# Gaps of 32 bytes between the weight blocks and between the x and g tiles of a fused attention and MLP kernel

## The chip, the core and the metric

The kernel runs on one core of one Trainium2 chip. The metric is the device time of one execution in microseconds; the kernel before has a median of 677.18 us over 3 runs (677.18 to 677.52). The instruction profile is of one further execution, which has a span of its own.

## What is computed

Sliding-window attention with sink tokens (4 batches, 8 heads, 768 positions, head dimension 64, 4 sinks, window 128), and behind it an MLP of 512 by 2048 with a leaky activation, over all 3072 tokens, in float32:

```python
scores = scale * np.matmul(q, k.transpose(0, 1, 3, 2))
keep = is_sink | in_window                    # rel = query - key position, 0 <= rel < window
scores = np.where(keep, scores, -1000000000.0)
a = np.exp(scores - max); a = a / (sum(a) + 1e-09)
x = np.matmul(a, v)                           # heads laid side by side: 3072 x 512
h = x @ w_in                                  # 512 x 2048
g = np.maximum(h, 0.0) + alpha * np.minimum(h, 0.0)
out = g @ w_out                               # 2048 x 512
```

## The kernel before, in words

The 3072 tokens are cut into 12 chunks of 256 (`NCHUNK`, three to a batch). The MLP's inner dimension of 2048 is cut into 16 blocks of 128, `f` = 0 to 15 (`NF`).

Each weight block f is one tile of 8192 bytes a partition in the memory of the core. It arrives as 64-bit floats in 32-bit words (`load_weights`), and is turned (`convert_weights`) into four parts of 512 float32 columns: high and low part of w_in, and high and low part of w_out. The converted block takes the place of the raw one (the same `tag`), so a block lies where its load was put. All 16 blocks stay in memory to the end. The memory of the last three (f = 13, 14, 15) is first lent to the input tiles of chunk 0 and to small tables, and is handed to the weights later; the dictionary `lent` names these three.

Attention of a chunk leaves its output transposed in two tiles, `xh` (its high part) and `xl` (the rest), each of 4 x 256 columns. There are two of each kind, used in turn by the chunks.

The MLP of a chunk goes through its 16 blocks:
- `gemm1(c, f)`, line L894: twelve matmuls of 256 columns. For each of four slices of the 512 inputs, w_in's high part is multiplied with xh and with xl, and its low part with xh. The weights are the stationary operand, x is the moving one. The result is in a PSUM bank.
- the activation: ACT scales the bank by alpha (L898), DVE takes the larger of the two (L899) into `g`, ACT rounds it into `gh` (L900), DVE writes the rest to `gl` (L901). There are three tiles each of gh and gl, used in turn by the blocks.
- `gemm2(c, f)`, lines L931, L932 and L929: six matmuls of 512 columns. Here gh or gl (128 columns of it) is the stationary operand and w_out's parts are the moving one: for each of the two halves of the tokens, gh with w_out's high part (L931) and its low part (L932), then for each half gl with the high part (L929). They add into two PSUM banks, over all 16 blocks.

`gemm2` runs two blocks behind `gemm1` (`LAG`). The attention of the next chunk is spread over the first twelve blocks of the present one, between its products; its scores are the matmuls L597 and L598. The last chunk has no attention beside it. Ahead of its block f = 8, the function `judge` begins, a test of whether the inputs allow this fast path; a single transpose of it is on TensorE (L1048).

The order of the instructions on each engine is made when the kernel is built: `Plan.draw` simulates the engines with estimated costs, and `Plan.issue` emits the operations in that order. Costs and order don't depend on where tiles lie.

Memory of the core is handed out by two pools, `const` (weights and what stays to the end) and `main` (`pool` in the code, all else of the fast path), in the order in which tiles are first asked for, each tile in one run of bytes, the same in every partition. A tile's place is then the sum of the sizes before it, each rounded up to 32 bytes. The helper `several` asks for the n tiles of a kind.

The places of the operands of the two products in the kernel before, modulo 128 bytes: the weight blocks 32, but 64 for f = 14; xh, xl, g, gh and gl all 96.

Of the kernel before, what the change touches and what calls it, by code (L numbers as in the profile page):

```python
# [3 lines left out]

# [5 lines left out]
F32 = mybir.dt.float32  # L10
F32R = mybir.dt.float32r
# [8 lines left out]
P = 128  # L20
# [4 lines left out]
QC = 2 * P  # L25
# [4 lines left out]
KT = DM // P  # L30
LAG = 2
# [47 lines left out]
class Plan:  # L79
# [20 lines left out]
    def held(self, tile_):  # L100
        v = Value(None)
        v.at = tile_
        return v

    def op(self, engine, cost, run, reads=(), writes=(), tail=0.09, mode=None, nbytes=0, other=None, locks=False):
        o = Op(engine, cost, tail, run, self.rank if engine == "PE" else None)
        o.ways = {engine: (cost, run)}
        if other:
            o.ways[other[0]] = other[1:]
        o.born = self.rank  # L110
        if engine == "PE":
            self.rank += 1
        o.mode, o.nbytes, o.index = mode, nbytes, len(self.ops)
        seen = []
        for group, writing in ((reads, False), (writes, True)):
            for x in group:
                v, key = x if isinstance(x, tuple) else (x, None)
                if v not in seen:
                    seen.append(v)
                keys = [k for k in set(v.wrote) | set(v.read) if key is None or k is None or k == key]  # L120
                for k in keys:
                    o.before.update(v.wrote.get(k, ()))
                    if writing:
                        o.before.update(v.read.get(k, ()))
                if writing:
                    for k in keys:
                        if key is None or k == key:
                            v.wrote.pop(k, None)
                            v.read.pop(k, None)
                    v.wrote.setdefault(key, []).append(o)  # L130
                else:
                    v.read.setdefault(key, []).append(o)
        for v in seen:
            v.left += 1
        o.values = seen
        o.takes = [v for v in seen if v.kind]
        o.locks = locks
        self.ops.append(o)
        return o
# [182 lines left out]
def program(ctx, tc, qk, pairs, vp, vq, vs, w, par, out):  # L322
    nc = tc.nc
    const = ctx.enter_context(tc.tile_pool(name="const", bufs=1))
    fast = ctx.enter_context(ExitStack())
    pool = fast.enter_context(tc.tile_pool(name="main", bufs=1))
    psum = ctx.enter_context(tc.tile_pool(name="psum", bufs=1, space=bass.MemoryType.PSUM))
    plan = Plan(tc)
# [3 lines left out]
    for name, which in (("s", (0, 1)), ("pa", (2, 3)), ("h", (4, 5)), ("o", (6, 7))):  # L332
        plan.kind(name, [banks[i] for i in which])

    def several(name, n, shape, dtype):
        plan.kind(name, [pool.tile(shape, dtype, name=f"{name}{i}") for i in range(n)])

    scratch = ctx.enter_context(tc.tile_pool(name="scratch", bufs=1, space=bass.MemoryType.DRAM))
    plan.kind("swap", [scratch.tile([4, P, P], F32, name=f"swap{i}") for i in range(2)])
    plan.kind("turns", [scratch.tile([4, P, 2 * 32], F32, name=f"turns{i}") for i in range(2)])  # L340
    trid = held(scratch.tile([P, 2, P], F32, name="trid"))
    several("stage", 2, [P, QC + KC], F32)
    several("kq", 2, [P, KC + 2 * QC], F32R)
    several("v", 4, [P, 3, 2, D], F32)
    several("pt_", 3, [P, 2, WIN], F32)
    several("comb", 5, [P, 4 * P], F32)
# [7 lines left out]
    several("sinkT", 1, [P, QC], F32R)  # L354
    several("vs", 1, [P, DM], F32R)
    several("ob", 2, [P, DM], F32)
    several("xh", 2, [P, KT, QC], F32R)
    several("xl", 2, [P, KT, QC], F32R)
    several("g", 2, [P, QC], F32)
    several("gh", LAG + 1, [P, QC], F32R)  # L360
    several("gl", LAG + 1, [P, QC], F32R)

    size = const.tile([P, NF], F32, name="size")
    sizes = held(size)
# [2 lines left out]
    def load_weights(f, engine="ACT"):  # L367
        raw = raws[f] = held(None)

        def run():  # L370
            raw.at = const.tile([P, 2 * DM, 2], I32, tag=f"w{f}", name="wraw")
            (nc.sync if engine == "SP" else nc.scalar).dma_start(
                raw.at.rearrange("p (i x) w -> p i (x w)", i=2), w[f].bitcast(I32).rearrange("i p x -> p i x"))
        return op(engine, ISSUE if engine == "SP" else 0.12, run, writes=[raw] + lent.get(f, []), nbytes=8 * P * 2 * DM)
# [35 lines left out]
    lent = {}  # L410
# [136 lines left out]
    xh, xl, prep, comb, sink, ptile_, sums, rinv, nms, wt = {}, {}, {}, {}, {}, {}, {}, {}, {}, {}  # L547
# [730 lines left out]
```

## Time and profile before

| | |
|---|---|
| median of 3 runs | 677.18 us |
| profiled execution, span | 676.2 us |
| TensorE matmul busy | 663.8 us (98%), 4532 matmuls |
| weight loads busy (beside the matmuls) | 580.5 us (86%), 4534 |
| VectorE busy | 525.8 us (78%) |
| ScalarE busy | 397.5 us (59%) |
| mean granted TensorE clock | 0.994 |
| DMA | 85.19 MB, 126 GB/s in the mean |

A share of busy time counts an instruction from its start to its end. Matmuls overlap on TensorE: the next starts while the one before is still draining, so the sum of their durations is larger than the time they take up, and the pace is read from the distance of their starts. In the page's rows "bank<-xh,w" stands for a matmul that writes a PSUM bank and reads x and w; "x1536" is the count; behind the bar stand busy microseconds, the mean nanoseconds of one, and the idle time before them with what ended it. PEld rows are the loads of the stationary operand. In a timeline row the first number is the start in microseconds from the start of the span, the second the time to the end of what the row merges, and "x1" the count of instructions.

### The profile page before, as it was taken

The page shows a single profiled execution, that of the slowest core. Times are in us where ns is not written, and L with a number is a line of the kernel's source. Part 1 is how long each engine was busy: PE and PEld are TensorE (multiplying, and loading weights), DVE is VectorE, ACT ScalarE, POOL GpSimd, SP SyncE. Part 2 cuts the span into 40 slices and gives each one's busy share as a digit, 9 for nine tenths or more (in the row PEclk, how much of TensorE's full clock was granted, in tenths as well). Part 3 has the DMA queues.
Part 4 walks back from the last instruction along what each step waited for, and adds up shares of the span by engine and source line. Part 5 has one row for each costly group of instructions (what it writes and reads, how often), then busy time and mean ns, then how long its engine had stood idle before and what let it go on. Part 6 is the DMA issues. An engine that isn't in the chain of part 4 may idle for free.

```text
span 676.2 us, 13243 instructions
## 1 busy us (share of the span) xinstructions
PE 663.8 (98%) x4532; PEld 580.5 (86%) x4534; DVE 525.8 (78%) x1750; ACT 397.5 (59%) x1066; POOL 34.5 (5%) x115
## 2 busy tenths in 40 slices
PE   9989999999999999999999999999999999999996
PEld 4577898888989989989988988988998988998995
DVE  6999999968967976986986995995895994994331
ACT  6989888827636726736636735644744753853332
POOL 2110000001000000000000000010000000000000
PEclk9979999999999999999999999999999999999999
DMA  8684641424343453443443433552542543420001
GB/s 314 229 277 151 241 187 39 127 71 147 122 133 107 122 148 93 145 132 95 141 118 114 143 107 93 163 140 61 172 128 78 161 128 88 142 94 17 32 2 35
DMA packets 58683, 85.19 MB, mean 126 GB/s; under 512 B 9072, under 2 KB 35056, under 8 KB 58608
## 3 DMA queue, kind: packets, MB, share of 16 engines
q1 hardware_dynamic: 55056, 71.17, 34.7%
q10 hardware_dynamic: 3552, 13.11, 5.4%
q8 instruction: 37, 0.61, 0.4%
q14 instruction: 38, 0.31, 0.1%
HBM read 67.22 MB, written 17.04 MB: 125 GB/s over the span
## 4 chain that ended last, share of the span: by engine, by line
PE 83%; DVE 9%; ACT 5%; issue 2%; POOL 0%; DMA 0%; ACTq 0%; SPq 0%; POOLq 0%
PE bank L894 35%; PE bank L931 12%; PE bank L932 11%; PE bank L929 11%; PE bank L786 3%; PE bank L598 3%; PE bank L597 3%; PE bank L875 2%; DVE wa L396 2%; ACT pt L614 1%; ACT wa L382 1%; DVE wa L394 1%; DVE w L404 1%; DVE g L899 1%; DVE gl L901 1%
## 5 line engine op out<-in xcount | busy, mean ns | idle before, releaser
L894 PE MATMUL bank<-xh,w 128*128 128x256 f32 x1536 | 307.9, 283 | 0.4 <-DVE g L899 0.2
L894 PEld LDWEIGHTS bank<-xh,w 128*128 128x128 f32 x1536 | 250.6, 189 | 9.0 <-DVE g L899 3.0
L894 PE MATMUL bank<-xl,w 128*128 128x256 f32 x768 | 215.1, 280 | 0.1
L898 ACT ACTIVATE g<-bank,param 128x256 f32<-128x256 f32 x192 | 90.5, 472 | 117.4 <-PE bank L894 113.1
L931 PE MATMUL bank<-w,gh 128*128 128x512 f32 x382 | 151.7, 397 | 0.2 <-ACT gh L900 0.2
L932 PE MATMUL bank<-w,gh 128*128 128x512 f32 x382 | 150.1, 393 | 0.0
L894 PEld LDWEIGHTS bank<-xl,w 128*128 128x128 f32 x768 | 145.2, 189 | 4.4 <-DVE xl L808 0.3
L614 ACT ACTIVATE pt<-pt,nm 128x260 f32<-128x260 f32 (+1 forms) x192 | 94.5, 493 | 53.5 <-DVE nm L610 53.1
L899 DVE TENSOR_TENSOR g<-bank,g 128x256 f32<-128x256 f32 x192 | 79.7, 419 | 51.4 <-ACT g L898 50.9
L929 PE MATMUL bank<-w,gl 128*128 128x512 f32 x382 | 119.5, 394 | 0.0
L900 ACT CAST gh<-g 128x256 fp32r<-128x256 f32 x192 | 76.9, 404 | 59.7 <-DVE g L899 59.6
L901 DVE TENSOR_TENSOR gl<-g,gh 128x256 fp32r<-128x256 f32 x192 | 80.5, 423 | 26.5 <-ACT gh L900 23.0
L610 DVE CUSTOM_DVE_ANT_0 pt<-bank,masks 128x260 f32<-128x260 f32 (+1 forms) x192 | 75.0, 401 | 19.3 <-PE bank L598 15.5
L929 PEld LDWEIGHTS bank<-w,gl 128*128 128x128 f32 x382 | 70.7, 188 | 16.2 <-issue 0.7
L931 PEld LDWEIGHTS bank<-w,gh 128*128 128x128 f32 x382 | 71.9, 188 | 9.5 <-ACT gh L900 0.7
L932 PEld LDWEIGHTS bank<-w,gh 128*128 128x128 f32 x382 | 71.9, 188 | 8.3
L563 DVE TENSOR_TENSOR kq<-stage,kq 64x392 fp32r<-64x392 f32 x80 | 45.3, 566 | 2.7
L659 POOL TENSOR_TENSOR sink<-pt,ri 128x8 f32<-128x8 f32 x80 | 20.8, 264 | 504.7 <-DVE ri L644 358.8
L597 PE MATMUL bank<-kq 128*128 128x260 f32 (+1 forms) x160 | 44.4, 278 | 1.3 <-DVE nm L610 1.3
L598 PE MATMUL bank<-kq 128*128 128x260 f32 (+1 forms) x160 | 45.0, 281 | 0.0
L655 DVE CUSTOM_DVE_ANT_0 comb<-pt,ri 128x128 f32<-128x128 f32 x136 | 43.1, 343 | 0.4
L561 ACT CAST kq<-stage 128x392 fp32r<-128x392 f32 x80 | 40.9, 512 | 0.7 <-ACT pt L614 0.2
(130 smaller groups left out, 686.9 us busy)
## 6 DMA issues: line engine op xcount, KB each, us to landing
stage<-qk SPq DMA_DIRECT2D x80, 324.0 KB, 2.9
wraw<-w ACTq DMA_DIRECT2D x12, 1024.0 KB, 5.9
swap<-comb SPq DMA_DIRECT2D x36, 256.0 KB, 2.0
comb<-swap SPq DMA_DIRECT2D x36, 256.0 KB, 3.2
v<-vq SPq DMA_DIRECT2D x36, 192.0 KB, 2.5
out_dram<-ob SPq DMA_DIRECT2D x22, 256.0 KB, 3.5
wraw<-w SPq DMA_DIRECT2D x4, 1024.0 KB, 12.0
v<-vp SPq DMA_DIRECT2D x8, 192.0 KB, 6.9
```

What stands on the lines that cost most here:

```text
L597: nc.tensor.matmul(s[:, w0], qh()[:, qs], ks()[:, kw], start=True, stop=False)
L598: nc.tensor.matmul(s[:, w0], ql()[:, qs], ks()[:, kw], start=False, stop=True)
L610: op("DVE", dve(n), lambda: nc.vector.tensor_tensor_reduce(out=pt.at[:, u, w0], in0=s.at[:, w0], in1=masks[:, i, w0], scale=-0.125, scalar ...
L614: op("ACT", exp(n), lambda: nc.scalar.activation(pt.at[:, u, w0], pt.at[:, u, w0], AF.Exp, bias=nm.at[:, h, u:u + 1], scale=-1.0, accum_ou ...
L894: nc.tensor.matmul(h(), fin.at[:, 0, part, ks], rhs.at[:, kt], start=(kt == 0 and n == 0), stop=(kt == KT - 1 and n == 2))
L898: op("ACT", act(QC, True), lambda: nc.scalar.activation(g.at, h(), AF.Copy, scale=alt[:, f:f + 1]), reads=[bk, known("param")], writes=[g])
L899: op("DVE", dve(QC), lambda: nc.vector.tensor_tensor(g.at, h(), g.at, ALU.max), reads=[bk], writes=[g])
L900: op("ACT", cast(QC), lambda: nc.scalar.copy(gh.at, g.at), reads=[g], writes=[gh])
L901: op("DVE", dve(QC), lambda: nc.vector.tensor_tensor(gl.at, g.at, gh.at.bitcast(F32), ALU.subtract), reads=[g, gh], writes=[gl])
L929: nc.tensor.matmul(o2[j].at, gl.at[:, js], fin.at[:, 1, 0], start=False, stop=(f == NF - 1))
L931: nc.tensor.matmul(o2[j].at, gh.at[:, js], fin.at[:, 1, 0], start=(f == 0), stop=False)
L932: nc.tensor.matmul(o2[j].at, gh.at[:, js], fin.at[:, 1, 1], start=False, stop=False)
```

## The change

Tiles that nothing reads or writes are asked for between the others: 32 bytes (8 floats) a partition between the two xh tiles, between the two xl tiles, between the three gh and between the three gl tiles, and between the last gh and the first gl; 96 bytes between xh and xl; and 32 bytes ahead of each weight block whose memory wasn't lent (f = 0 to 12). The instructions of every engine, their order and their waits are the same as before; what differs is the addresses of tiles.

```diff
+    gaps = count()
+
+    def gap(where, n=8):
+        where.tile([P, n], F32, tag=f"gap{next(gaps)}", name="gap")
+
-    def several(name, n, shape, dtype):
-        plan.kind(name, [pool.tile(shape, dtype, name=f"{name}{i}") for i in range(n)])
+    def several(name, n, shape, dtype, between=()):
+        tiles = []
+        for i in range(n):
+            if i and between:
+                gap(pool, between[i - 1])
+            tiles.append(pool.tile(shape, dtype, name=f"{name}{i}"))
+        plan.kind(name, tiles)
...
-    several("xh", 2, [P, KT, QC], F32R)
-    several("xl", 2, [P, KT, QC], F32R)
+    several("xh", 2, [P, KT, QC], F32R, (8,))
+    gap(pool, 24)
+    several("xl", 2, [P, KT, QC], F32R, (8,))
     several("g", 2, [P, QC], F32)
-    several("gh", LAG + 1, [P, QC], F32R)
-    several("gl", LAG + 1, [P, QC], F32R)
+    several("gh", LAG + 1, [P, QC], F32R, (8, 8))
+    gap(pool)
+    several("gl", LAG + 1, [P, QC], F32R, (8, 8))
...
         def run():
+            if f not in lent:
+                gap(const)
             raw.at = const.tile([P, 2 * DM, 2], I32, tag=f"w{f}", name="wraw")
```

The places modulo 128 bytes, before and after:

| tile | before | after |
|---|---|---|
| w, f = 0 to 12 | 32 | 64, 96, 0, 32 and so on in turn |
| w, f = 13, 14, 15 | 32, 64, 32 | 64, 64, 32 |
| xh, of even and of odd chunks | 96, 96 | 0, 32 |
| xl, of even and of odd chunks | 96, 96 | 0, 32 |
| gh, the three | 96, 96, 96 | 32, 64, 96 |
| gl, the three | 96, 96, 96 | 0, 32, 64 |

All tiles of attention (stage, kq, v, pt_, comb, wa, sinkT, vs, ob, masks, tri) lie 32 bytes further on modulo 128, those of `const` ahead of the weights where they were.

More of the change, by code (lines that the diff above doesn't have):

```diff
@@ L3 @@
 from contextlib import ExitStack
+from itertools import count
 import concourse.bass as bass
```

## The prediction

> **What bounds the kernel now.** I read the page first, for the engine that sets the end, and its chain of waits.
>
> ```profile
> span 676.2 us, 13243 instructions
> PE 663.8 (98%) x4532; PEld 580.5 (86%) x4534; DVE 525.8 (78%) x1750; ACT 397.5 (59%) x1066; POOL 34.5 (5%) x115
> PE 83%; DVE 9%; ACT 5%; issue 2%; POOL 0%; DMA 0%; ACTq 0%; SPq 0%; POOLq 0%
> L894 PE MATMUL bank<-xh,w 128*128 128x256 f32 x1536 | 307.9, 283 | 0.4 <-DVE g L899 0.2
> L894 PEld LDWEIGHTS bank<-xh,w 128*128 128x128 f32 x1536 | 250.6, 189 | 9.0 <-DVE g L899 3.0
> L894 PE MATMUL bank<-xl,w 128*128 128x256 f32 x768 | 215.1, 280 | 0.1
> L931 PE MATMUL bank<-w,gh 128*128 128x512 f32 x382 | 151.7, 397 | 0.2 <-ACT gh L900 0.2
> L597 PE MATMUL bank<-kq 128*128 128x260 f32 (+1 forms) x160 | 44.4, 278 | 1.3 <-DVE nm L610 1.3
> L598 PE MATMUL bank<-kq 128*128 128x260 f32 (+1 forms) x160 | 45.0, 281 | 0.0
> ```
>
> TensorE is busy for 98% of the span and holds 83% of the chain, and before the two large products it is idle for 0.4 and 0.2 us in all. So the time is the number of matmuls times the distance at which one starts after another. The 283 ns of a row is not that distance (they overlap); it has to be read from starts. As many weight loads as matmuls are listed: each matmul runs while the stationary operand of the next is being read.
>
> Second, the timeline of TensorE in the last chunk, where there is no attention left and only two blocks alternate: the twelve 256-column matmuls of the first product (L894) and the six 512-column ones of the second (L931, L932, L929). The second product runs two blocks behind, so the last L931 row below belongs to f=14 and the one before it to f=13, while the L894 rows at 662.10 and 664.89 begin f=14 and f=15.
>
> ```profile
> 639.61 0.28 PE L894 MATMUL bank<-xh,w 128*128 128x256 f32 x1
> 642.37 0.28 PE L894 MATMUL bank<-xh,w 128*128 128x256 f32 x1
> 643.76 0.39 PE L931 MATMUL bank<-w,gh 128*128 128x512 f32 x1
> 645.14 0.27 PE L1048 MATMUL bank<-ident,worst 128*1 128x128 f32 x1
> ...
> 648.05 0.28 PE L894 MATMUL bank<-xh,w 128*128 128x256 f32 x1
> 649.47 0.40 PE L931 MATMUL bank<-w,gh 128*128 128x512 f32 x1
> 650.86 0.28 PE L894 MATMUL bank<-xh,w 128*128 128x256 f32 x1
> ...
> 662.10 0.28 PE L894 MATMUL bank<-xh,w 128*128 128x256 f32 x1
> 663.50 0.40 PE L931 MATMUL bank<-w,gh 128*128 128x512 f32 x1
> 664.89 0.28 PE L894 MATMUL bank<-xh,w 128*128 128x256 f32 x1
> 666.27 0.39 PE L931 MATMUL bank<-w,gh 128*128 128x512 f32 x1
> 667.64 0.40 PE L931 MATMUL bank<-w,gh 128*128 128x512 f32 x1
> 669.05 0.39 PE L916 MATMUL bank<-w,gh 128*128 128x512 f32 x1
> ```
>
> Here is the fact on which everything rests. A pair of blocks takes 642.37 - 639.61 = 2.76 us before the one odd transpose L1048, and 650.86 - 648.05 = 2.81 us after it: the same instructions, with nothing awaited. The extra 0.05 us (1.8%) stays for the pairs that follow. The other engines don't explain it:
>
> ```profile
> 631.33:642.37 11.04, 11.04 (x73) 10.06 (x72) 3.40 (x8) 3.52 (x9) 0.00 (x0) 1.00 0.03 12
> 648.05:659.28 11.23, 11.23 (x73) 10.16 (x72) 3.40 (x8) 3.53 (x9) 0.00 (x0) 1.00 0.01 2
> ```
>
> Each of these windows (columns: length, busy PE, weight loads, DVE, ACT, POOL, granted clock, DMA share, GB/s) holds four pairs, 73 matmuls with the one at its edge. DVE, ACT and DMA do the same in both and the clock is 1.00 in both; yet one takes 11.04 us and the other 11.23. So TensorE has two paces, and which it is in is inherited from what ran before. The same pair of paces stands in the middle of the kernel:
>
> ```profile
> 425.59 0.28 PE L894 MATMUL bank<-xh,w 128*128 128x256 f32 x1
> 426.95 0.28 PE L597 MATMUL bank<-kq 128*128 128x260 f32 x1
> 427.19 0.40 PE L931 MATMUL bank<-w,gh 128*128 128x512 f32 x1
> 428.58 0.28 PE L597 MATMUL bank<-kq 128*128 128x260 f32 x1
> 428.82 0.28 PE L894 MATMUL bank<-xh,w 128*128 128x256 f32 x1
> 430.24 0.28 PE L597 MATMUL bank<-kq 128*128 128x260 f32 x1
> ```
>
> A first-product block took 426.95 - 425.59 = 1.36 us (113 ns a matmul), the next 430.24 - 428.82 = 1.42 us (118 ns), a second-product block between them 428.58 - 427.19 = 1.39 us. A clash of the two reads that TensorE makes at once, the moving operand of one matmul and the stationary operand of the next, would look like this: either they miss each other and keep missing, or they meet and keep meeting.
>
> **The change part by part.** No instruction, wait or queue entry is added or removed, and each engine's list is the same; the gaps are tiles that nothing writes. What changes is where operands lie. Let the distance be the place of the next stationary operand minus that of the current moving one, modulo 128 bytes, summed from the sizes of the tiles as they are laid out. Before, every x, gh and gl tile lies at 96 and every weight block at 32, so the distance is 64 in both products. One block is an exception: f=14 lies at 64, because its memory starts behind other small tiles, and has the distances 96 (first product) and 32 (second). After, the weight blocks lie at 64, 96, 0, 32 and so on in turn (f=13 and 14 at 64, f=15 at 32), x at 0 in even chunks and at 32 in odd ones, gh at 32, 64, 96, gl at 0, 32, 64. So the distances 0, 32, 64 and 96 all occur. In the first product 7 of 16 blocks of an even chunk and 9 of 16 of an odd one are at 32 or 96: 96 of 192 blocks. In the second, gh and gl of one number lie 32 apart, so that either the gh loads or the gl loads of each block are at 32 or 96: about half, 96 blocks' worth of 192.
>
> Block f=14 is therefore the experiment that the profile already contains. Its first product took 663.50 - 662.10 = 1.40 us; other blocks took 1.36 (fast), 1.38 (f=15: 666.27 - 664.89) and 1.42 (slow). Its second product took 669.05 - 667.64 = 1.41 us, against 667.64 - 666.27 = 1.37 for f=13 and 1.39 in the slow pace. At a distance of 32 or 96 it has neither of the two paces of distance 64, but one near the slow one, or above it.
>
> The sum. How much of the kernel runs at which pace no view adds up, so I take half and half: 1.39 us for the first product (of 1.36 and 1.42), 1.38 for the second (of 1.37 and 1.39), 2.77 a pair.
> - First product, 96 blocks to 1.40: 96 x 0.01 = +1.0 us. From below, all of the changed blocks could find the fast pace (96 x -0.03 = -2.9), from above, all the slow one (96 x 0.03 = +2.9).
> - Second product, 96 blocks' worth to 1.41 would be 96 x 0.03 = +2.9; since in each block only part of the loads has the distance of f=14, and each switch between gh and gl shifts the two reads against each other in a direction that I can't tell, I take +2.4. From below 96 x -0.01 = -1.0; from above the same loss on all blocks, 192 x 0.03 = +5.8.
> - Blocks at distance 0: no block of before stays there. I take them to be like 64. From below 96 x (2.73 - 2.77) = -3.8, from above 96 x (2.83 - 2.77) = +5.8, between the fastest and the slowest blocks seen.
> - Attention: its tiles all shift by the same 32 bytes, so that distances within it stay; nothing. If that is wrong, the 320 matmuls of L597 and L598 at 5 ns (118 against 113) would be 1.6 us.
> - DVE and ACT read and write tiles at other places. Their work on g stands two blocks (over 5 us) ahead of the matmuls that need it, and the waits (columns: the total, times, longest, in us) show how little TensorE stands on them:
>
> ```profile
> PE bank L588 <- DVE nm L610: 1.7, 2, 1.2
> PE bank L931 <- ACT gh L900: 0.2, 1, 0.2
> PE bank L894 <- DVE g L899: 0.2, 1, 0.2
> ```
>
> Nothing, therefore; 5% on all of DVE's 525.8 us would still leave it under TensorE.
>
> Together +3.4 us: a span of 676.2 + 3.4 = 679.6. The median of the runs, 677.18, lies 1.0 over the profiled span, which gives 680.6 us.
>
> The Trainium skill ("TensorE: Matmul & The Clock Gate", section "Step-by-step: what each phase is for") says against all this that loading the next weights uses a read port of its own and takes nothing from the running matmul. By that rule places can't matter and the time stays, which is the first rival below; the trace's two paces at an equal clock are not what the rule leads one to expect, but they prove no clash of addresses either.
>
> **The rivals.**
> 1. Places don't matter, and f=14 is slow by what ran before it. For it: the pace does depend on the past, as L1048 shows; f=14 is one block. Against: it falls on neither pace. Then the mixture stays, within 1 us: 677.2 us. This also stands for gains and losses that cancel.
> 2. Faster: the changing distance breaks the slow pace. Now it lasts as long as nothing disturbs it, as after L1048 (648.05 to 662.10, five pairs, 2.81 each). If from f to f the two reads start with another distance, slow spells could end within a block, and the fast pace be found again. For it: block f=15 took 1.38 us straight behind blocks of 1.42 and 1.40 with no odd instruction between, while the way from fast to slow took one. Against: the f=14 block. It decides if over half of the blocks come to 2.76 or less: with all pairs at 2.75, 192 x -0.02 = -3.8, 673.4 us; with all at 1.36 + 1.37 = 2.73, 192 x -0.04 = -7.7, 669.5 us.
> 3. Much slower: the switch between gh and gl, or between blocks, meets a clash each time. With all blocks at the slowest seen, 1.42 + 1.41 = 2.83, 192 x 0.06 = +11.5, 688.7 us. Against: every loss would have to last.
> 4. That the gaps don't move anything (rounding of sizes, or reuse of the places): the layout is as given above, and excludes it.
>
> **How the numbers follow.** My forecast, slower by 1.4 to 7 us, 0.47; rival 1, 0.20; rival 2, 0.27; rival 3, 0.06. Predicted is the forecast's 680.6 us. What can be told from no change is 0.2%, 1.4 us. So slower 0.53, within 0.2% 0.20, faster 0.27. Since both signs are in play, the range reaches from 668 (rival 2 with a little beyond its end) to 687 (most of rival 3); that of the forecast alone is 678.6 to 684.
>
> **What would show it.** In the last chunk of the changed kernel, pairs of blocks should differ from f to f, with first-product blocks of 1.40 us wherever the distance is 32 or 96, and second-product blocks of 1.39 to 1.41, and no run of equal pairs that lasts until a disturbance. Wrong: pairs still at 2.76 or 2.81 throughout (rival 1), or pairs at 2.75 and below in most of the last chunk and in the middle (rival 2). The count of instructions, the waits of TensorE and its clock should be the same; a longer wait for ACT or DVE would mean that I had the wrong engine.

## The result, and the profile after

The changed kernel takes 681.47 us in the median of 4 runs (681.33 to 681.69), against 677.18 us before: a ratio of 1.0061, with a 95% interval of 1.0047 to 1.0075. It is slower by 4.3 us, where 3.4 were forecast. The profiled span went from 676.2 to 679.8 us, by 3.6.

The page of the changed kernel (L909 is what L894 was, L946, L947 and L944 are L931, L932 and L929, L914 and L915 are L899 and L900):

```profile
span 679.8 us, 13245 instructions
PE 667.4 (98%) x4534; PEld 583.6 (86%) x4534; DVE 526.6 (77%) x1750; ACT 398.8 (59%) x1066; POOL 34.7 (5%) x115
PE 89%; ACT 4%; DVE 4%; issue 1%; POOL 0%; DMA 0%; ACTq 0%; SPq 0%; POOLq 0%
L909 PE MATMUL bank<-xh,w 128*128 128x256 f32 x1536 | 311.5, 284 | 0.4 <-DVE g L914 0.2
L909 PE MATMUL bank<-xl,w 128*128 128x256 f32 x768 | 216.0, 281 | 0.1
L946 PE MATMUL bank<-w,gh 128*128 128x512 f32 x382 | 151.3, 396 | 0.2 <-ACT gh L915 0.2
```

All 3.6 us of the span are on TensorE (663.8 to 667.4 us busy, two matmul records more in the trace); VectorE and ScalarE differ by about 1 us (525.8 to 526.6, 397.5 to 398.8) and the idle time ahead of the two products is the same 0.4 and 0.2 us. The rows of the first product grew (307.9 to 311.5 and 215.1 to 216.0), the row of L946 shrank a little (151.7 to 151.3). The mean granted clock, 0.996, is not lower than the 0.994 of before. So the time did not come from a wait, nor from the clock.

The waits of TensorE in the changed kernel (total, times, longest, in us) say the same:

```profile
PE bank L603 <- DVE nm L625: 2.2, 2, 1.2
PE bank L946 <- ACT gh L915: 0.2, 1, 0.2
PE bank L909 <- DVE g L914: 0.2, 1, 0.2
```

The timeline of TensorE in the last chunk, with the first matmul of each first-product block. The odd transpose (L1063, before L1048) stands just ahead of 648.66:

```profile
631.82 0.28 PE L909 MATMUL bank<-xh,w 128*128 128x256 f32 x1
634.63 0.28 PE L909 MATMUL bank<-xh,w 128*128 128x256 f32 x1
637.43 0.28 PE L909 MATMUL bank<-xh,w 128*128 128x256 f32 x1
640.24 0.28 PE L909 MATMUL bank<-xh,w 128*128 128x256 f32 x1
...
651.55 0.28 PE L909 MATMUL bank<-xh,w 128*128 128x256 f32 x1
654.37 0.28 PE L909 MATMUL bank<-xh,w 128*128 128x256 f32 x1
657.17 0.28 PE L909 MATMUL bank<-xh,w 128*128 128x256 f32 x1
```

Pairs of blocks now take 2.81, 2.80 and 2.81 us ahead of the transpose, and 2.82 and 2.80 behind it. The stretch of 2.76 us a pair that the kernel before has there is gone; about the 2.81 us that it has behind L1048 is now everywhere. The windows of four pairs (columns as before) show the same at the same work of VectorE and the same clock (ScalarE has two instructions more in the first):

```profile
631.82:643.04 11.22, 11.22 (x74) 10.18 (x72) 3.40 (x8) 4.49 (x11) 0.00 (x0) 1.00 0.14 48
651.55:662.79 11.24, 11.24 (x74) 10.16 (x73) 3.40 (x8) 3.54 (x9) 0.00 (x0) 1.00 0.01 2
```

11.22 us against 11.04 ahead of the transpose, 11.24 against 11.23 behind it.

For the whole kernel I took the starts of successive matmuls from the trace, and subtracted. Summed over all steps of the first product that the traces have (2289 of them in each), the time from start to start rose from 272.1 to 275.4 us, **+3.3 us**; over the second's (1139) from 266.3 to 267.0, **+0.7 us**; all else is 0.5 us shorter. The mean undisturbed step (up to a quarter longer than the shortest) rose from 116.2 to 118.0 ns in the first product and from 231.2 to 232.0 in the second. These two means, taken in this way, are used for every kernel below. The blocks show it one by one: of the first-product blocks with no disturbed step, the kernel before has 141, from 1.36 to 1.43 us, 77 of them below 1.40; the changed kernel has 142, all from 1.40 to 1.44 us.

### The profile page after: what moved, and what is told of

It is laid out like the page before. It is cut to its first block, busy times and chain, and to the rows that moved or that the text cites. A ratio compares the mean times of both kernels' runs of the same rounds, so it can differ in the third digit from the quotient of the medians.

```text
span 679.8 us, 13245 instructions
## 1 busy us (share of the span) xinstructions
PE 667.4 (98%) x4534; PEld 583.6 (86%) x4534; DVE 526.6 (77%) x1750; ACT 398.8 (59%) x1066; POOL 34.7 (5%) x115
## 4 chain that ended last, share of the span: by engine, by line
PE 89%; ACT 4%; DVE 4%; issue 1%; POOL 0%; DMA 0%; ACTq 0%; SPq 0%; POOLq 0%
PE bank L909 39%; PE bank L946 13%; PE bank L944 12%; PE bank L947 12%; PE bank L801 3%; PE bank L613 3%; PE bank L612 3%; PE bank L890 2%; ACT pt L629 1%; ACT wa L397 1%; DVE wa L411 1%; PE bank L874 1%; ACT w L416 1%; PE bank L603 1%; DVE pt L625 0%
## 5 line engine op out<-in xcount | busy, mean ns | idle before, releaser
L909 PE MATMUL bank<-xh,w 128*128 128x256 f32 x1536 | 311.5, 284 | 0.4 <-DVE g L914 0.2
L909 PEld LDWEIGHTS bank<-xh,w 128*128 128x128 f32 x1536 | 250.9, 189 | 9.1 <-DVE g L914 2.8
L909 PE MATMUL bank<-xl,w 128*128 128x256 f32 x768 | 216.0, 281 | 0.1
L946 PE MATMUL bank<-w,gh 128*128 128x512 f32 x382 | 151.3, 396 | 0.2 <-ACT gh L915 0.2
L947 PE MATMUL bank<-w,gh 128*128 128x512 f32 x382 | 150.4, 394 | 0.0
L909 PEld LDWEIGHTS bank<-xl,w 128*128 128x128 f32 x768 | 145.1, 189 | 4.5 <-DVE xl L823 0.3
L914 DVE TENSOR_TENSOR g<-bank,g 128x256 f32<-128x256 f32 x192 | 79.8, 419 | 52.6 <-ACT g L913 51.7
L944 PE MATMUL bank<-w,gl 128*128 128x512 f32 x382 | 120.1, 395 | 0.0
L915 ACT CAST gh<-g 128x256 fp32r<-128x256 f32 x192 | 77.1, 405 | 58.6 <-DVE g L914 58.3
L944 PEld LDWEIGHTS bank<-w,gl 128*128 128x128 f32 x382 | 70.6, 188 | 16.3 <-issue 0.7
L946 PEld LDWEIGHTS bank<-w,gh 128*128 128x128 f32 x382 | 71.8, 188 | 9.6 <-ACT gh L915 0.6
L947 PEld LDWEIGHTS bank<-w,gh 128*128 128x128 f32 x382 | 71.8, 188 | 8.5
```

Of the source, the lines that this page charges most:

```text
L909: nc.tensor.matmul(h(), fin.at[:, 0, part, ks], rhs.at[:, kt], start=(kt == 0 and n == 0), stop=(kt == KT - 1 and n == 2))
L914: op("DVE", dve(QC), lambda: nc.vector.tensor_tensor(g.at, h(), g.at, ALU.max), reads=[bk], writes=[g])
L915: op("ACT", cast(QC), lambda: nc.scalar.copy(gh.at, g.at), reads=[g], writes=[gh])
L944: nc.tensor.matmul(o2[j].at, gl.at[:, js], fin.at[:, 1, 0], start=False, stop=(f == NF - 1))
L946: nc.tensor.matmul(o2[j].at, gh.at[:, js], fin.at[:, 1, 0], start=(f == 0), stop=False)
L947: nc.tensor.matmul(o2[j].at, gh.at[:, js], fin.at[:, 1, 1], start=False, stop=False)
```

## The experiments

Sums, prices and "modulo 128" in the expectations are those that I held when the run was sent. Distance stands for the place of the next stationary operand minus that of the current moving one. The kernels with gaps use the `gap` and `several` of the change. Each ratio is taken against runs of the kernel before from the same session, whose median went from 677.31 to 678.50 us, and not against 677.18.

### Only the weight blocks

```diff
+    gap(pool, 152)
...
+            if f not in lent:
+                gap(const)
```

The gap of 608 bytes brings x, g and all behind them back to their places of before.

> Only the gaps ahead of the weight blocks are kept; xh, xl, gh and gl lie as in the kernel before (all at 96 modulo 128, xh and xl alike modulo 1024). The distance then changes from block to block and is the same within one. Theory A (the distance modulo 128 alone sets the pace; 32 and 96 are slow): half of all blocks lose, 1.0 us in the first product and 2.4 to 2.9 in the second, 680.6 us. Theory B (the loss of the changed kernel comes from xh and xl lying 128 bytes apart modulo 256, so that the place of the moving operand alternates from matmul to matmul, whatever it is modulo 128): the first product keeps its fast pace of 113 ns in the blocks at distance 0 and 64, 677.5 to 679 us. Theory C (places don't matter): 677.2 us.

681.56 us, ratio 1.0063 (1.0047 to 1.0080); first product 117.8 ns a step, second 232.8. The weight gaps alone cost as much as the whole change. xh and xl lie alike here, so theory B, which put the whole loss down to their lying 128 bytes apart, does not hold; theory A's sum (680.6) is near.

### Only the x tiles

```diff
-    several("xh", 2, [P, KT, QC], F32R)
-    several("xl", 2, [P, KT, QC], F32R)
+    several("xh", 2, [P, KT, QC], F32R, (8,))
+    gap(pool, 24)
+    several("xl", 2, [P, KT, QC], F32R, (8,))
+    gap(pool, 216)
```

> Only the gaps among the x tiles are kept (32 bytes between the two xh and the two xl, 96 between xh and xl); behind them a gap fills up to 1024 bytes, so that g, gh and gl lie as before, and the weights aren't moved. Theory A: even chunks stay at distance 64, odd ones come to 32; 96 blocks of the first product lose 0.01 us each, the second product nothing: 678.2 us. Theory B (xh and xl 128 bytes apart modulo 256): the first product loses its fast pace everywhere, 116.1 to 118 ns a matmul over 2304 of them, +4.2 us: 681.4 us. Theory C: 677.2 us.

679.74 us, ratio 1.0038 (1.0026 to 1.0051); first product 117.7 ns, second 230.8, a little under its 231.2 of before. That lies between theory A's 678.2 and theory B's 681.4. The parts don't add up (0.63% and 0.38% against 0.61% together): each alone brings the first product to about the pace of the whole change (117.8 and 117.7 ns against 118.0).

### Places modulo 128 as before, xl moved by 128 bytes

If the place modulo 128 bytes were what counts, as the prediction has it, this kernel should take the time of before.

```diff
     several("xh", 2, [P, KT, QC], F32R)
+    gap(pool, 32)
     several("xl", 2, [P, KT, QC], F32R)
+    gap(pool, 224)
```

> The kernel before with one gap of 128 bytes between the xh tiles and the xl tiles, filled up to 1024 behind them: every place modulo 128 is what it was, only xh and xl now differ by 128 modulo 256. Theory A: no change, 677.2 us, and blocks of 12 matmuls at 1.36 and 1.42 us as before. Theory B: the fast pace of the first product is lost, +4.2 us, 681.4 us. Theory C: 677.2 us.

680.14 us, ratio 1.0043 (1.0026 to 1.0060); first product 117.8 ns, second 230.7. The last chunk of this kernel, first matmul of successive blocks:

```profile
635.09 0.28 PE L907 MATMUL bank<-xh,w 128*128 128x256 f32 x1
637.88 0.28 PE L907 MATMUL bank<-xh,w 128*128 128x256 f32 x1
640.67 0.28 PE L907 MATMUL bank<-xh,w 128*128 128x256 f32 x1
```

2.79 us a pair where the kernel before has 2.76, with every place modulo 128 unchanged. So 128 bytes is not the period, and the prediction's distances were taken in the wrong measure. Modulo 256 bytes, x and g lay at 224 and the weights at 32 (f=14 at 192): distances 64 and 192. Here the steps on xl are at 192 instead of 64.

### The patterns of matmuls by themselves

A kernel that leaves out attention and the MLP and runs only blocks like theirs on data loaded once, eight times for each distance, each time behind one odd matmul of 128 to 142 columns, which shifts the moment at which the block starts. ScalarE, VectorE and the DMA queues have next to nothing to do meanwhile, and the granted clock is 1.00 over the blocks. Each kernel of this kind ran once.

```python
odd(s)                                     # one matmul of s = 128, 130, ... 142 columns
...
n = 0
for kt in range(4):
    k = W + d + kt * P                     # d: the distance
    for lo, x in ((0, 0), (0, 1), (1, 0)):
        m = X + x * (1024 + e) + kt * QC   # e: xl moved against xh
        nc.tensor.matmul(bk, big[:, k + lo * DM:k + lo * DM + P], big[:, m:m + QC], start=n == 0, stop=n == 11)
        n += 1
```

> No attention and no MLP: only the two patterns of matmuls, with operands at chosen places in one tile (the output is a copied PSUM bank). For each setting eight blocks as in the kernel, each behind one odd matmul of 128 to 142 columns that shifts the moment at which the block begins. First product: distance of weights and x from 0 to 512 bytes with xh and xl alike, then xl moved against xh by 32 to 256 bytes. Second product: distance of gh and w from 0 to 256 bytes, then gl moved against gh. Theory A: at 64 the blocks take 1.36 or 1.42 us (second product 1.37 or 1.40) by where they begin, at 32 and 96 about 1.40 (1.41), and the pattern repeats after 128 bytes; xl moved by 128 or 256 bytes changes nothing. Theory B: with xl moved by 128 bytes no block stays at 113 ns a matmul; the pattern may repeat only after 256 bytes or more. Theory C: every setting has the same two paces.

Mean ns of a step over the eight blocks, without the steps next to the odd matmul (the first three and the last of a block in the first product, the first and the last in the second). Distances that several of these kernels share came out within 0.4 ns of each other in the first product and within 0.8 in the second.

| distance, bytes | 0 | 32 | 64 | 96 | 128 | 160 | 192 | 256 | 512 |
|---|---|---|---|---|---|---|---|---|---|
| first product | 119.2 | 118.0 | 116.1 | 117.8 | 118.9 | 119.5 | 117.7 | 119.1 | 119.0 |
| second product | 229.7 | 232.6 | 233.1 | 232.3 | 231.7 | 234.5 | 230.9 | 229.1 | |

At distance 64 with xl moved by 128 the first product took 118.2, by 256 again 116.2; with xl moved by 128 at distances 0 and 32 it took 117.8 both times. At 256 and 512 the steps are those of 0 to within 0.2 ns in the first product. Distances that are alike modulo 128 differ: 64 and 192 (116.1 and 117.7), 32 and 160 (118.0 and 119.5). So the places of the two operands matter on TensorE by itself, and in the first product the distance 64 of the kernel before is the best of those listed. The timeline of this kernel, one row a block (x12) with the odd matmul between: two blocks at distance 0, then three at distance 64.

```profile
37.47 1.64 PE L53 MATMUL bank<-big 128*128 128x256 f32 x12
38.95 0.23 PE L39 MATMUL bank<-big 128*128 128x142 f32 x1
39.01 1.64 PE L53 MATMUL bank<-big 128*128 128x256 f32 x12
40.49 0.22 PE L39 MATMUL bank<-big 128*128 128x128 f32 x1
...
78.76 1.63 PE L53 MATMUL bank<-big 128*128 128x256 f32 x12
80.22 0.23 PE L39 MATMUL bank<-big 128*128 128x132 f32 x1
80.28 1.60 PE L53 MATMUL bank<-big 128*128 128x256 f32 x12
81.72 0.23 PE L39 MATMUL bank<-big 128*128 128x134 f32 x1
81.78 1.62 PE L53 MATMUL bank<-big 128*128 128x256 f32 x12
83.25 0.23 PE L39 MATMUL bank<-big 128*128 128x136 f32 x1
```

At distance 0 a block takes 38.95 - 37.47 = 1.48 us, both times. At 64 it takes 1.46, 1.44 and 1.47: fast behind the odd matmul of 132 columns, slow behind those of 130 and 134, and so in turn through all eight. The same block at the same places has two paces, and the moment of its start picks one. The kernel before has two paces of the same kind; here they stand without any other engine.

### The first product at one distance, 0

If the loss came from distances that change from block to block, a kernel with one distance throughout should be as fast as before.

```diff
+    pool.tile([P, 16], F32, name="gapa")
     several("xh", 2, [P, KT, QC], F32R)
     several("xl", 2, [P, KT, QC], F32R)
+    pool.tile([P, 240], F32, name="gapb")
```

> The kernel before with all x tiles moved on by 64 bytes (a gap of 64 ahead of xh, filled up to 1024 behind xl): one distance for the whole first product, 0 instead of 64 (f=14: 160 instead of 224), the same for all blocks and both chunks' tiles; the second product isn't touched. Theory A (modulo 128, with 0 like 64): 677.2 us. Theory D: 119.2 ns a matmul instead of 116.2 over 2304, +6.9 us: 684 us, slower than the changed kernel although no distance varies. Theory E (it is the variety of distances that costs, by breaking the fast pace): no loss, 677.2 us.

683.08 us, ratio 1.0068 (1.0049 to 1.0087): slower than the changed kernel. First product 119.3 ns a step (119.2 where the distance is 0, the figure of the patterns alone), second 230.9. The last chunk:

```profile
635.24 0.28 PE L896 MATMUL bank<-xh,w 128*128 128x256 f32 x1
638.07 0.28 PE L896 MATMUL bank<-xh,w 128*128 128x256 f32 x1
640.90 0.28 PE L896 MATMUL bank<-xh,w 128*128 128x256 f32 x1
```

2.83 us a pair. The distance itself does it; it need not change. Theory D had it (684), theories A and E (no loss) are excluded.

### The second product at one distance, 0

```diff
     several("xl", 2, [P, KT, QC], F32R)
+    pool.tile([P, 16], F32, name="gap")
     several("g", 2, [P, QC], F32)
```

> The kernel before with g, gh and gl moved on by 64 bytes: the distance of the second product is 0 modulo 256 instead of 192, the first product isn't touched. Theory A: 0 is like 64, 677.2 us. Theory D: the second product at 229.7 ns instead of 230.9 where the beginnings are spread evenly, -1.4 us, and up to -5 us where it keeps the 226.6 ns that some beginnings find: 672 to 676 us, faster than both kernels. Theory C: 677.2 us.

677.36 us over 10 runs, ratio 0.9992 (0.9981 to 1.0003). The second product went from 231.2 to 229.2 ns a step, as the patterns had it (229.7), but the first from 116.2 to 116.7 at unchanged places. By 1152 and 2304 steps that is -2.3 and +1.1 us; the interval of the time, -1.3 to +0.2 us, does not tell it from no change, and theory D's 672 to 676 was missed. In the last chunk its pairs settle at 2.77 us, ahead of the odd transpose and behind it.

### Finer distances, and a kernel made from the best two

Two more kernels of patterns alone, at all distances from 0 to 252 in steps of 4 bytes.

> The matmul patterns alone, at distances from 0 to 248 bytes in steps of 8 (and some of 4), eight beginnings each, xh and xl and gh and gl alike. Theory D (the pace follows the distance modulo 256, not 128; formed after the first four runs): in the first product a fast pace of 113 ns only near a distance of 64, elsewhere 117 to 120; in the second 226 to 232 near 0, 230 to 234 elsewhere, 231 at 192. Theory A (modulo 128): the second half of the range repeats the first. Theory C: no dependence.

> The matmul patterns alone, at the distances that are 4 modulo 8, from 4 to 252 bytes. Theory D: the paces vary as they do at multiples of 8, between 113 and 121 ns in the first product and 226.6 and 235 in the second; 76 again at about 114.2 in the first and 120 at about 228 in the second, which are measured once more. Some of the new distances may be better.

First product: 114.2 at 76 in both kernels, 115.9 at 168, 116.0 at 64, 116.1 at 88, all others between 116.3 and 121.3. Second: 227.2 at 156, 227.8 at 132, 227.9 at 120, 229.0 and 229.7 at 240 in the two kernels, 229.4 at 216, the others 230.2 to 236.8. The upper half of the range does not repeat the lower one (76: 114.2, 204: 120.7), so that 128 bytes is not the period here either. Neighbouring distances, 4 bytes apart, differ by up to 7 ns (156 and 160 in the second product, 227.2 and 234.1), with no rule that I could see.

A kernel with distances 76 and 120 everywhere, f=14 too, by slices that start inside larger tiles:

```diff
+    pool.tile([P, 56], F32, name="gapx")
+    xs = pool.tile([P, 4 * KT * QC + 8], F32R, name="xs")
+    xs = [xs[:, 5 + i * KT * QC:5 + (i + 1) * KT * QC].rearrange("p (k x) -> p k x", k=KT) for i in range(4)]
...
+    pool.tile([P, 40], F32, name="gapg")
+    gs_ = pool.tile([P, 2 * (LAG + 1) * QC + 8], F32R, name="gs")
+    gs_ = [gs_[:, 6 + i * QC:6 + (i + 1) * QC] for i in range(2 * (LAG + 1))]
...
+    const.tile([P, 40], F32, name="gapw")
```

> The kernel before with places taken from the table of the matmul patterns alone: x 76 bytes and g -120 bytes modulo 256 from the weights (distance 76 in the first product, 120 in the second, all 16 weight blocks alike, f=14 too), by way of slices that begin inside two larger tiles. Order and waits as before. Theory D (the pace follows the distance modulo 256): 114.2 instead of 116.2 ns over 2304 matmuls, -4.6 us, and 227.9 instead of 231.0 over 1146, -3.6 us: about 669 us. If the beginnings that the kernel happens to have are worse than the eight of the table, as in the kernel with g moved by 64: 669 to 675 us. Theory A (modulo 128) has no reason for a gain: 677 us or more.

684.74 us, ratio 1.0104 (1.0087 to 1.0121). The second product came out faster (229.9 ns), the first much slower (120.7 instead of 114.2). So the distance is not the whole of it either: here the moving x starts at 116 bytes modulo 256, in the patterns at 160.

### The place of the moving operand at a fixed distance

> The matmul patterns alone. First, distances 64 and 76 (first product) and 156, 120 and 192 (second) with the moving operand itself moved by 0 to 212 bytes, so that the distance stays. Theory D (distance modulo 256 alone): every place gives the pace of its distance (116.0, 114.2, 227.2, 227.9, 231). Theory F (formed after the kernel with distances 76 and 120 came out slower: the place of the moving operand counts too, since it began at 116 there and at 160 in the table): the pace of the distance holds where the moving operand is shifted by a multiple of 32 bytes, and at a shift of 212 bytes, as in that kernel, distance 76 gives about 120. Last, pairs of blocks in turn without anything between, x at 224 and w at 32 as in the kernel before: at distance 192 of the second product 2.76 or 2.81 us a pair, as in the last chunk; at 0, 156, 120, 132 and 216 less where the second product keeps 227 ns: 12 x 113.3 + 6 x 227 = 2.72 us.

Mean ns of a step of the first product, with x and the weights moved together from their place in the first kernel of patterns (x at 160 modulo 256):

| both moved by, bytes | 0 | 4 | 8 | 12 | 16 | 20 | 32 | 64 | 128 | 212 |
|---|---|---|---|---|---|---|---|---|---|---|
| distance 64 | 116.4 | 121.0 | 120.3 | 117.8 | 114.8 | 119.9 | 117.3 | 116.0 | 115.1 | 119.8 |
| distance 76 | 114.2 | 120.8 | 120.0 | 117.9 | 118.6 | 121.4 | 116.1 | 114.6 | 113.9 | 120.7 |

The column 212 has the places of the kernel above, and its 120.7 ns is what that kernel took. Where the moving operand starts at a multiple of 16 bytes the step takes 114 to 119 ns, elsewhere in this table 118 to 121. So theory D fails, and theory F holds only in part: a shift by 32 bytes should keep the pace, and at distance 76 it costs 1.9 ns. In the second product it fails: at distance 156 the step takes 227.9 ns unmoved, but 237.8 and 239.1 with both operands moved by 32 and 64 bytes. The timeline where the shift goes from 0 to 4 at distance 76 in the first product:

```profile
207.01 1.58 PE L55 MATMUL bank<-big 128*128 128x256 f32 x12
208.43 0.23 PE L41 MATMUL bank<-big 128*128 128x140 f32 x1
...
211.50 1.67 PE L55 MATMUL bank<-big 128*128 128x256 f32 x12
213.00 0.23 PE L41 MATMUL bank<-big 128*128 128x130 f32 x1
```

1.42 us a block (six of the eight at shift 0 take 1.42 to 1.43, two 1.45 to 1.46), then 1.50. In the same kernel twenty pairs of blocks in turn, with the first product at 64, settled at 2.760 us a pair with the second at 192 (the distances and the fast pace of the kernel before), and at 2.773 with 0 (as in the last chunk of the kernel with g moved by 64), 2.780 with 132, 2.793 with 120, 2.813 with 216, and 2.725 and 2.875 in turn with 156. What a block does hangs on the one before it, so the best blocks don't make the best pairs, and none of these beat the combination of before; the 2.72 us that was expected came only in every second pair of 156.

### Only the g tiles, and xl moved by 256 bytes

Two kernels that the account so far has to foretell: the remaining part of the change, and the gap between xh and xl at twice its size.

```diff
-    several("gh", LAG + 1, [P, QC], F32R)
-    several("gl", LAG + 1, [P, QC], F32R)
+    several("gh", LAG + 1, [P, QC], F32R, (8, 8))
+    gap(pool)
+    several("gl", LAG + 1, [P, QC], F32R, (8, 8))
```

> Only the gaps among the gh and gl tiles; the weight blocks and the x tiles lie as before, so every distance of the first product is 64 as before (f=14 apart), and the distances of the second product are spread over 0 to 224 modulo 256. Theory (each product pays for its own distances, by the paces read so far): second product +0.8 ns on 1146 steps = +0.9 us, first product unchanged at 116.2 ns a step, so 1.0 us over the kernel before, ratio 1.001 to 1.002. Rival 1, the prediction's own term: +2.4 us, ratio 1.0035, all of it in steps of L931, L932 and L929. Rival 2 (the pace of the first product hangs on the moment at which it starts, and uneven second-product blocks between its blocks take the fast pace from it): first product at 117 to 118 ns although its places are those of before, +1.8 to +4.0 us there, ratio 1.004 to 1.007.

677.40 us over 12 runs, ratio 0.9998 (0.9987 to 1.0009). Second product 231.7 ns (+0.5), first 115.7 (-0.5, at unchanged places). The gaps among the g tiles cost nothing that can be measured, which speaks against both rivals. It is not quite the account's either: the second product rose by 0.5 of the 0.8 ns expected, but the first did not stay as it was, and the ratio lies under the 1.001 to 1.002 that was expected. As in the kernel with g moved by 64, a change of the second product's places alone moved the pace of the first; that it does so by the moment at which the first starts is likely, and not shown.

```diff
     several("xh", 2, [P, KT, QC], F32R)
+    gap(pool, 64)
     several("xl", 2, [P, KT, QC], F32R)
+    gap(pool, 192)
```

> As the kernel with one 128-byte gap between the xh tiles and the xl tiles, but with 256 bytes there (and 768 behind the xl tiles, so that all that follows moves by 1024 bytes in both). Theory (the period is 256 bytes): every step as in the kernel before, first product 116.2 ns a step, ratio 1.000 with the interval across it. Rival 1 (a longer period, 512 bytes or more, or any displacement of xl against xh loses the fast pace): first product at 117.7 ns a step as with the 128-byte gap, +3 us, ratio 1.004. Rival 2 (what cost time in the kernel with the 128-byte gap was the 1024 bytes by which all other tiles had moved): the same 1.004.

677.26 us over 11 runs, ratio 0.9993 (0.9984 to 1.0003); 116.2 and 231.2 ns, the figures of the kernel before. Its last chunk:

```profile
633.06 0.28 PE L907 MATMUL bank<-xh,w 128*128 128x256 f32 x1
635.82 0.28 PE L907 MATMUL bank<-xh,w 128*128 128x256 f32 x1
638.58 0.28 PE L907 MATMUL bank<-xh,w 128*128 128x256 f32 x1
641.34 0.28 PE L907 MATMUL bank<-xh,w 128*128 128x256 f32 x1
644.13 0.36 PE L907 MATMUL bank<-xh,w 128*128 128x256 f32 x1
647.02 0.28 PE L907 MATMUL bank<-xh,w 128*128 128x256 f32 x1
649.83 0.28 PE L907 MATMUL bank<-xh,w 128*128 128x256 f32 x1
```

2.76 us three times, then 2.79 and 2.89 around the odd transpose, then 2.81: the pairs of the kernel before, step for step. With 128 bytes in that place it was 2.79 but for the pairs around the transpose. All other tiles moved by 1024 bytes here too, so this displacement was not what cost time there. That 256 bytes is a period is shown for xl in the kernel itself.

## Why the prediction was right, and where it wasn't

The direction, the engine and the mechanism in its broad sense held: nothing is awaited, places set the pace of TensorE, and the pace of before was a good one to lose. Of 3.4 us forecast 3.6 came in the span. Inside that sum two terms were mis-sized in opposite directions, and the measure behind both was wrong. That their errors cancelled to within 0.6 us is luck.

| term | predicted | measured |
|---|---|---|
| first product, 96 blocks to 1.40 us | +1.0 us | +3.3 us, all blocks |
| second product | +2.4 us | +0.7 us; the gaps of g alone nothing |
| distance 0 like 64 | 0 | 119.2 against 116.1 ns a step where it is everywhere |
| attention | 0 | steps of its scores 121.4 ns in both kernels |
| VectorE, ScalarE | 0 | waits of TensorE the same |

- **The distance modulo 128 bytes** is the step that failed. It rested on no row: in the trace of before only the distances 64 and that of f=14 occur, and a period can't be read from two points. The kernel with xl moved by 128 bytes costs 0.43%, the one with 256 nothing. Modulo 256 the change spreads the first product over eight distances, not four, with xh and xl 128 bytes apart; so distances that the prediction left at the pace of 64 (0 and 64 modulo 128) lost too, and no undisturbed block stayed below 1.40 us.
- **"Blocks at distance 0 ... I take them to be like 64"** failed for the same reason: the kernel with distance 0 throughout is the slowest of those that moved x alone by gaps, at 2.83 us a pair, the figure that the prediction named as the slowest.
- **The first product's +1.0 us** was made from 1.40 us at f=14 against a half-and-half mixture of 1.36 and 1.42. The mean of before is 116.2 ns a step, 12 x 116.2 = 1.39 us, as the mixture had it. After, it is 12 x 118.0 = 1.42 us, and all blocks lie near it: the upper bound of the term (+2.9 us) was nearer than the value taken, and covered too few blocks.
- **The second product's +2.4 us** took one block, f=14 at 1.41 us, for all blocks with a 32-byte step between gh and gl. f=14's own distances did average about 234 ns a step against 231.0, so the reading of that block was right; but the distances of the others are mostly not its distance, and the spread of them takes 232.0.
- **Rival 1** (places don't matter) is refuted by the patterns alone and by six kernels, the changed one among them, that differ from before only in places and are slower by 0.38 to 1.04%. **Rival 2** (changing distances break the slow pace) came out reversed: the last chunk shows that it is the fast pace that the change takes away. It was fed by the true observation that a run of equal pairs lasts until something disturbs it.
- **What would show it**: that pairs would differ from f to f was wrong for the changed kernel. But for the pair around the transpose they lie at 2.79 to 2.82 us throughout. There a first-product block has two distances in turn, 128 bytes apart, because xh and xl lie so, and with that the patterns took 117.8 to 118.2 ns at each of the three distances tried. The sign does appear in the kernel with the weight gaps alone, where a block has one distance. Its last chunk:

```profile
631.45 0.28 PE L908 MATMUL bank<-xh,w 128*128 128x256 f32 x1
634.29 0.28 PE L908 MATMUL bank<-xh,w 128*128 128x256 f32 x1
637.08 0.28 PE L908 MATMUL bank<-xh,w 128*128 128x256 f32 x1
639.89 0.28 PE L908 MATMUL bank<-xh,w 128*128 128x256 f32 x1
642.72 0.28 PE L908 MATMUL bank<-xh,w 128*128 128x256 f32 x1
```

Pairs of 2.84, 2.79, 2.81 and 2.83 us. In the mean over its chunks, without the steps at a block's edges, the first product takes 119.6 ns a step at f=2 (distance 160, in the patterns 119.5) and 115.7 at f=7 (distance 64, in the patterns 116.1). One block does not fit: f=3, at distance 192, takes 115.6 where the patterns have 117.7 and f=11, at the same distance, 118.1.

The Trainium skill ("TensorE: Matmul & The Clock Gate", section "Step-by-step: what each phase is for") says that loading the next weights takes no read bandwidth from the running matmul. With every other engine idle, the first product took 113.9 to 121.4 ns a step, in the mean over eight blocks, by the places of the two operands alone, so the trace does not agree with what it implies for the pace; that the two reads clash is the likely reading, but no run here shows the reads themselves.

What stays open: why the pace depends on the places in the pattern that it does, and why the last chunk of the kernel before does not return to 2.76 us behind the odd transpose, while the same pairs of patterns alone, started behind a matmul of 128 columns, settled at 2.760 us after one pair.

## What to carry to other kernels

In a kernel bound by back-to-back matmuls, the places of stationary and moving tiles are worth up to about 1% here (677.3 to 684.7 us), so a change that shifts allocations for another reason can gain or lose that much with no wait to show for it: compare the starts of successive matmuls in a stretch without other work before explaining a small difference. Start the moving operand at a multiple of 16 bytes, which here was needed for the best paces but not enough for them, and when testing places, move them in the kernel itself and by more than one candidate period, since what a block does alone did not tell what a pair of blocks does.

## What the runs showed of the hardware that was not expected

- The pace of a matmul stream depends on where its two operands lie relative to each other: 256 bytes between xh and xl changed nothing (0.9993), 128 bytes cost 0.43%, and distances of 0, 256 and 512 bytes gave 119.2, 119.1 and 119.0 ns a step. It also depends on where both lie: at distance 76 in the first product a common shift by 16 bytes took it from 114.2 to 118.6 ns.
- A moving operand that starts off multiples of 16 bytes took some 4 to 6 ns a step more in most cases (116.4 to 121.0 ns at distance 64 and 231.1 to 236.8 in the second product at distance 192, both moved by 4 bytes), though 12 bytes cost only 1.4 in the first.
- The same block at the same places takes one of two paces by the moment at which it starts. In the fast one the raw starts are 113.33 ns apart, which is 17 times 6.667 ns; in the slow one 117.78 ns in the mean. Put into seven groups by their start modulo 6.667 ns, the steps of the first product in the kernel before (without the first three and the last of a block) keep 51% of their variance within the groups; with 6.6 or 6.7 ns in its place they keep over 99%. A step that is a whole multiple would keep its moment, and so its pace. A block can change its pace on the way: the one that starts at 642.37 in the kernel before takes 0.59 us for its first five steps and 0.79 for its last seven. That the start matters is shown by the odd matmuls of the patterns; the 6.667 ns are a reading of the traces that no run tested.
